# A linear-attention and gated-MLP block: two output transposes joined, gate/up tasks halved, two weight slices moved

## The chip, the cores and the metric

The kernel runs on one core of a Trainium2 chip. The metric is the device time of one execution in microseconds (us), the median of several. The engines are named as the profile names them: PE (TensorE matmul), PEld (its weight loads), DVE (VectorE), ACT (ScalarE), POOL (GpSimd) and SP (SyncE, which here only issues DMAs).

## The reference

Sequence 2048, width 448, 16 heads of 28, inner width 1792, all in bfloat16:

```
n = layernorm(x);  q, k, v = split(n @ wqkv)
phi(t) = where(t > 0, t + 1, exp(t)) + 1e-6
kv = phi(k).T @ v and z = sum(phi(k)), per head
o = (phi(q) @ kv) / (phi(q) @ z + 1e-6)
h = x + o @ wo
m = layernorm(h)
out = h + (gelu(m @ w_gate) * (m @ w_up)) @ w_down
```

## The kernel before, in words

The sequence is cut into 16 tiles of 128 rows. Every piece of work is a task with a name, an engine, the buffers that it reads and writes, and from these its waits. The tasks of an engine run strictly in the order that a table of names, ORDERS (L14), gives for it: one string for PE, ACT, DVE, POOL and SP. A task at the head of its engine's queue that waits holds back everything behind it.

**Attention.** Per tile t: layernorm statistics on DVE (`bnst`, `bnag`), `ln` and `rstd` on ACT, `norm` on DVE or POOL, a transpose (`tr0` to `tr3` on PE with an evacuation `ev` on ACT, later tiles by DMA, `xT`). `k`, `v` (L561) are the two halves of a tile's key and value products; `ek` and `evv` on ACT, a clamp `cl` on POOL (L566) and `ph` on DVE (L568) make phi(k) and v, and `acc` adds the tile to the sum kv, which stays in two banks of PSUM. `qa`, `qb` (L606) are query products of two head groups for four tiles, evacuated by ACT (`eq`, `rq`: exponential and relu, L616, L617) and finished by DVE (`cq`, `pq`). When all tiles are in kv, DVE copies it out (`kz1`, `kz2`).

**From attention to the MLP.** Tiles 0 and 1 go by `a2_first` (L663): `nd` multiplies phi(q) with kv, DVE divides (`rd`, `om`) into `o_sb`, `tro` transposes the tile on PE, `evo` on ACT evacuates it, `wo` multiplies with wo, `hr` on DVE adds x, then layernorm, `trh` (seven transposes of hn on PE) and `evh`. The other tiles go in pairs by `a2_pair` (L711), with DMA transposes `oT` and `hT` on SP instead; DVE adds a copy of hn (`wrap`), and POOL computes the layernorm's factors and the norm.

**MLP.** `gu_chunk` (L788) makes gate and up for 2, 2, 4, 4 and 4 tiles. A task `gu` fills one pair of PSUM banks: two column blocks of 128 for chunks of two tiles, 28 matmuls, or one block for chunks of four, 14 matmuls. The pairs of banks alternate, so gu3 reuses those of gu1. Two `ge` on ACT apply gelu to the gate half, two `hm` on DVE multiply it with up. `down` multiplies two tiles with w_down, `out` adds h, `dout` stores.

**Halves of 64 rows.** Most matmuls contract only 64 rows, in pairs: one on array rows 0 to 63 into one bank, its partner on rows 64 to 127 into another (`pe_pairs`, L434). A task's second half (`v`, `qb`, `nd..b`, `wo..b`, `down..b`) uses the same two banks with the row halves exchanged, so it waits until the first half is complete. Tasks that use all 128 rows are the warm-up `warm0`, `nd0`, `nd1`, `tro`, most of `wo0` and `wo1`, `trh` and the last four tiles' `down`.

**Start.** 16 small and 38 further products of ones run on PE (`warm1`, `warm0`, L457) while the first x tiles arrive; they wait for `ones`, a POOL memset.

**Loads.** SP issues x, weights and DMA transposes from one queue. The gate and up weights come as seven slices of 64 rows each (`dwg0`, `dwu0`, ..., L536), all issued before the first `oT`; the down weights (`dwd`, L732) follow oT2 and oT3. A gate/up task reads slice k with its k-th pair of matmuls.

Of the kernel before, what the change touches and what calls it, by code (L numbers as in the profile page):

```python
# [912 lines left out]
```

## Time and profile before

| | |
|---|---|
| median of 3 runs | 196.69 us (196.25 to 196.73) |
| the profiled execution | 196.7 us |
| its span, first to last instruction | 194.9 us |
| PE busy in the span | 190.3 us (98%) |
| PE's granted clock over the span | 0.999 |
| from the first instruction to the first gate/up product | 54.13 us |

The span is the profiled program's own instructions; 1.8 us of the execution lie around it. In a timeline row stand the start from the span's first instruction, the length from there to the end of the last instruction in the row, engine, line, operation, what is written and read, shapes and count; the brackets tell idle time of the engine ahead of it and what ended it. Consecutive equal instructions share a row, so a step is read as the difference of two starts. Matmul ends overlap the next starts.

### The profile page before, as it was taken

What the parts mean: (1) busy time and instruction counts of PE and PEld (TensorE: products, weight loads), DVE (VectorE), ACT (ScalarE), POOL (GpSimd) and SP (SyncE); (2) the same over time, 40 slices, a digit from 0 to 9 for tenths busy, and PEclk for the clock granted to TensorE, in tenths of its full rate; (3) what the DMA queues carried; (4) which work ended last, traced back from release to release, by engine and by line L of the source; (5) the groups of instructions that cost most, each with busy time, mean ns of one, the idle gap of its engine ahead of it and who ended that gap; (6) DMA issues with size and microseconds to landing.
All of it is one profiled execution on the core that took longest, in us unless ns stands there. A gap on an engine that the chain in (4) does not pass through costs nothing.

```text
span 194.9 us, 5336 instructions
## 1 busy us (share of the span) xinstructions
PE 190.3 (98%) x2192; PEld 137.9 (71%) x2192; DVE 116.3 (60%) x301; ACT 78.2 (40%) x205; POOL 42.0 (22%) x90
## 2 busy tenths in 40 slices
PE   7999999999999999999999999999999999999994
PEld 7556658754588977976675577877778779899554
DVE  2989735368998946843967745756735443431512
ACT  3689866669784212220442441233232442411100
POOL 3099974300050310500500500500500000000000
PEclk9999999999999999999999999999999999999999
DMA  6944558999836052152062250172040000010111
GB/s 191 377 116 97 81 110 185 247 248 205 260 103 110 15 101 50 50 105 62 10 129 46 46 106 2 30 117 51 5 94 28 23 0 0 3 47 3 47 47 47
DMA packets 37256, 17.53 MB, mean 90 GB/s; under 512 B 28272, under 2 KB 36336, under 8 KB 37232
## 3 DMA queue, kind: packets, MB, share of 16 engines
q1 hardware_dynamic: 36352, 16.45, 36.8%
q10 hardware_dynamic: 880, 0.75, 1.2%
q8 instruction: 17, 0.28, 0.6%
q14 instruction: 7, 0.06, 0.1%
HBM read 8.72 MB, written 1.84 MB: 54 GB/s over the span
## 4 chain that ended last, share of the span: by engine, by line
PE 96%; issue 1%; ACT 1%; DVE 1%; POOL 0%; DVEq 0%; ACTq 0%; POOLq 0%
PE ps L430 87%; PE ps L780 6%; PE ps L454 2%; DVE x_sb L660 1%; PE ps L495 1%; ACT xn L617 1%; PE ps L681 0%; ACT xnT L523 0%; PE ps L672 0%; DVE x_sb L756 0%; POOL ones_bf L395 0%; POOL eps_t L398 0%; ACT pqT L616 0%; DVEq L196 0%; ACTq L196 0%
## 5 line engine op out<-in xcount | busy, mean ns | idle before, releaser
L430 PE MATMUL ps<-hnT,wgu_sb 64*128 64x512 bf16 (+1 forms) x980 | 90.4, 333 | 0.0
L430 PEld LDWEIGHTS ps<-hnT,wgu_sb 64*128 64x128 bf16 x980 | 64.5, 94 | 18.6 <-DVE hh L832 1.7
L830 ACT ACTIVATE gl<-ps 128x256 bf16<-128x256 f32 x112 | 36.9, 381 | 89.3 <-PE ps L430 88.2
L832 DVE TENSOR_TENSOR hh<-ps,gl 128x256 bf16<-128x256 f32 x112 | 42.5, 415 | 35.7 <-ACT gl L830 31.5
L430 PE MATMUL ps<-wd_sb,hh 64*128 64x448 bf16 x336 | 34.4, 349 | 0.0
L430 PEld LDWEIGHTS ps<-wd_sb,hh 64*128 64x128 bf16 x336 | 25.6, 94 | 6.2 <-DVE x_sb L756 0.2
L430 PE MATMUL ps<-wkv_sb,xnT 64*128 64x448 bf16 x192 | 22.4, 350 | 0.4 <-ACT xnT L523 0.4
L462 DVE BATCH_NORM_STATS2 st<-x_sb 128x6 f32<-128x448 bf16 x32 | 18.7, 611 | 2.6 <-DMA x_sb<-in_A_x_dram 2.6
L756 DVE TENSOR_TENSOR x_sb<-ps,x_sb 128x448 bf16<-128x448 f32 (+1 forms) x17 | 9.9, 591 | 16.6 <-PE ps L430 9.8
L474 POOL TENSOR_SCALAR ln<-mv 128x2 f32<-128x2 f32 x7 | 1.6, 223 | 75.0 <-DVE mv L463 74.9
L568 DVE SCALAR_TENSOR_TENSOR pk<-ps,tm 128x448 bf16<-128x448 f32 x16 | 9.8, 620 | 9.6 <-POOL tm L566 7.1
L430 PE MATMUL ps<-xnT,wq_sb 64*128 64x512 bf16 x112 | 14.9, 377 | 0.2 <-ACT xn L617 0.2
L430 PEld LDWEIGHTS ps<-wkv_sb,xnT 64*128 64x128 bf16 x192 | 10.1, 94 | 6.3 <-issue 0.8
L430 PE MATMUL ps<-wo_sb,oT 64*128 64x448 bf16 x98 | 12.1, 350 | 0.1
L660 DVE TENSOR_TENSOR x_sb<-ps,x_sb 128x448 bf16<-128x448 f32 x16 | 9.4, 618 | 4.6 <-PE ps L430 4.4
L780 PE MATMUL ps<-wd_sb,hh 128*128 128x448 bf16 (+1 forms) x70 | 10.8, 315 | 0.0
L566 POOL TENSOR_SCALAR tm<-e 128x448 bf16<-128x448 bf16 x16 | 8.9, 559 | 6.4 <-ACT e L565 5.5
L487 POOL TENSOR_SCALAR hn<-x_sb,nm,rs 128x448 bf16<-128x448 bf16 x14 | 10.0, 720 | 0.8 <-POOL rs L476 0.2
L565 ACT ACTIVATE e<-ps 128x448 bf16<-128x448 f32 x16 | 8.5, 541 | 3.5 <-PE ps L430 2.2
L780 PEld LDWEIGHTS ps<-wd_sb,hh 128*128 128x128 bf16 x70 | 6.7, 98 | 4.3 <-issue 0.4
L655 DVE TENSOR_TENSOR o_sb<-ps,rd 128x448 bf16<-128x448 f32 x16 | 9.4, 612 | 0.1
L570 ACT ACTIVATE v<-ps 128x448 bf16<-128x448 f32 x16 | 8.4, 542 | 2.1 <-PE ps L430 2.1
(69 smaller groups left out, 140.4 us busy)
## 6 DMA issues: line engine op xcount, KB each, us to landing
out_dram<-x_sb SPq DMA_DIRECT2D x15, 112.0 KB, 1.7
wgu_sb<-in_B_w_gate_dram SPq DMA_DIRECT2D x7, 224.0 KB, 6.1
wgu_sb<-in_B_w_up_dram SPq DMA_DIRECT2D x7, 224.0 KB, 6.4
wd_sb<-in_B_w_down_dram SPq DMA_DIRECT2D x1, 1568.0 KB, 8.3
x_sb<-in_A_x_dram SPq DMA_DIRECT2D x2, 448.0 KB, 5.3
wkv_sb<-in_A_wqkv_dram ACTq DMA_DIRECT2D x2, 336.0 KB, 3.7
x_sb<-in_A_x_dram SPq DMA_DIRECT2D x3, 224.0 KB, 4.2
wo_sb<-in_A_wo_dram SPq DMA_DIRECT2D x2, 336.0 KB, 4.4
```

Source lines behind the costliest of these rows:

```text
L430: ins = e.matmul(o_, l_, r_, start=s_, stop=p_, **kw)
L462: op("dve", lambda e: e.bn_stats(st[:, t, :], src_ap), [b_src], [b_st[t]], "%sbnst%d" % ("" if mv is mv1 else "h", t), 0.53, key, after=after)
L487: return lambda e: e.tensor_scalar(dst, src[:, t, :], nm[:, t:t + 1], rs[:, t:t + 1], ALU.add, ALU.mult)
L565: act_exp(lambda e: e.activation(e1[:, ie, :], oK, AF.Exp), bank(bk), [b_e1[ie]], "ek%d" % t, _c_act(D), kk)
L566: op("pool", lambda e: e.tensor_scalar(tm1[:, ie, :], e1[:, ie, :], 1.0 + EPS, 0.0, ALU.min, ALU.max), [b_e1[ie]], [b_tm1[ie]], "cl%d" % t ...
L568: op("dve", lambda e: e.scalar_tensor_tensor(pk[:, i, :, 0:GW], psK3, EPS, tm1[:, ie, :].rearrange("p (g e) -> p g e", g=NG), ALU.max, ALU ...
L655: op("dve", lambda e: e.tensor_tensor(o_sb[:, so, oc:oc + D].rearrange("p (a e) -> p a e", e=28), nd3[:, :, 0:28], rd[:, i, :].unsqueeze(2 ...
L660: op("dve", lambda e: e.tensor_tensor(h_sb[:, u, :], ps[:, b, 0:D], x_sb[:, u, :], ALU.add), bank(b) + [b_x[u]], [b_h[u]], "hr%d" % u, 0.5 ...
L756: op("dve", lambda e: e.tensor_tensor(x_sb[:, t, c0:c1], ps[:, bk, c0:c1], h_sb[:, t, c0:c1], ALU.add), bank(bk) + [b_h[t]], [bo], "out%d% ...
L780: ins = e.matmul(ps[:, bk, c0:c1], hh[:, j, hsl(t)], wd_sb[:, j, c0:c1], start=(j == 0), stop=(j == NJ - 1))
L830: G.add("act", lambda e, gi=gi, cs_=cs_, psG=psG: e.activation(gl[:, gi, cs_], psG[:, cs_], AF.Gelu_apprx_tanh), r=bank(BK_G[i]), w=[b_glh ...
L832: op("dve", lambda e, dst=dst, srcU=srcU, srcL=srcL: e.tensor_tensor(dst, srcU, srcL, ALU.mult), bank(BK_U[i]) + [b_glh], [b_ar[j_][t % HR ...
```

## The change

- `tro0` and `tro1` become one task (`tro_first`): sixteen transposes in eight 64-row pairs. Rows 0 to 63 of both tiles go to one bank, rows 64 to 127 to the other. The task waits for `om0` and `om1`; `evo0` and `evo1` each read both banks and wait for all sixteen.
- A gate/up task of two column blocks becomes two tasks, a and b, of 14 matmuls each, in the same order of matmuls. `ge` and `hm` still wait for the second.
- Slices 5 and 6 of the gate and up weights are issued behind oT2 and oT3, and the down weights behind those.
- `trh` waits for the wrap copy only at its seventh transpose, the one that reads it.
- Clamps `cl14` and `cl15` run on DVE instead of POOL. `warm0` has 33 products instead of 38.
- ORDERS is a new table. At the start, `ones` on POOL stands behind `eps`, `mhalf` and `opad` (a memset of `o_sb`) instead of first; `rstd3` on ACT stands behind `ek0` and `ln4`, `tr3` on PE behind `v1`. In the hand-over, `qb31` stands behind the hn transposes instead of between `wo2a` and `wo2b`, and `cq14` on DVE behind `hm3`. In the last chunk gu54 and gu55 stand behind both halves of down10.

PE around the o transposes, before (the rows are nd2a, tro0, nd2b, then qb30 with qa21, tro1, qb21; kvz with pqT is `nd`, wq_sb is `qa` or `qb`):

```order
L430 MATMUL ps<-kvz,pqT 128x116 x8
L681 MATMUL ps<-ident,o_sb 128x128 x4
L430 MATMUL ps<-kvz,pqT 128x116 x8
L430 MATMUL ps<-xnT,wq_sb 128x512 x14
L681 MATMUL ps<-ident,o_sb 128x128 x4
L430 MATMUL ps<-xnT,wq_sb 128x512 x6
```

The same place of the changed kernel, up to the first products of wo1:

```order
L433 MATMUL ps<-kvz,pqT 128x116 x8
L693 MATMUL ps<-ident,o_sb 128x64 x16
L433 MATMUL ps<-kvz,pqT 128x116 x8
L433 MATMUL ps<-xnT,wq_sb 128x512 x20
L709 MATMUL ps<-wo_sb,oT 128x448 x3
```

The second group of o transposes is gone from between qa21 and qb21, and the sixteen stand where the first four did.

PE from qa31 to the fourth gate/up task, before (wo_sb is `wo`, ident with hn is `trh`, wgu_sb is `gu`):

```order
L430 MATMUL ps<-xnT,wq_sb 128x512 x8
L430 MATMUL ps<-wo_sb,oT 128x448 x8
L430 MATMUL ps<-xnT,wq_sb 128x512 x6
L430 MATMUL ps<-wo_sb,oT 128x448 x6
L702 MATMUL ps<-ident,hn 128x128 x14
L430 MATMUL ps<-kvz,pqT 128x116 x16
L430 MATMUL ps<-hnT,wgu_sb 128x256 x140
L430 MATMUL ps<-wo_sb,oT 128x448 x14
L430 MATMUL ps<-hnT,wgu_sb 128x256 x28
```

and in the changed kernel:

```order
L433 MATMUL ps<-xnT,wq_sb 128x512 x8
L433 MATMUL ps<-wo_sb,oT 128x448 x14
L725 MATMUL ps<-ident,hn 128x128 x14
L433 MATMUL ps<-xnT,wq_sb 128x512 x6
L433 MATMUL ps<-kvz,pqT 128x116 x16
L433 MATMUL ps<-hnT,wgu_sb 128x256 x140
L433 MATMUL ps<-wo_sb,oT 128x448 x8
L433 MATMUL ps<-hnT,wgu_sb 128x256 x14
L433 MATMUL ps<-wo_sb,oT 128x448 x6
```

wo2a and wo2b are now adjacent, qb31 (the six wq_sb products) follows the hn transposes, and half of gu4 stands between wo4a and wo4b.

DVE between the evacuation of hnT (`evh1`) and the products of the first two gate/up tasks, before (rd and o_sb are tiles 4 and 5, hh is `hm`, the row on pqT is `cq14`):

```order
L709 COPY hnT<-ps 128x7x128
L618 TENSOR_SCALAR pqT<-pqT 112x2x512
L462 BN_STATS st<-x_sb 128x6
L654 RECIPROCAL rd<-ps 128x16
L462 BN_STATS st<-x_sb 128x6
L654 RECIPROCAL rd<-ps 128x16
L463 BN_AGGR mv<-st 128x2 x2
L655 TENSOR_TENSOR o_sb<-ps,rd 128x448
L832 TENSOR_TENSOR hh<-ps,gl 128x256 x2
L655 TENSOR_TENSOR o_sb<-ps,rd 128x448
L832 TENSOR_TENSOR hh<-ps,gl 128x256 x2
```

and in the changed kernel:

```order
L732 COPY hnT<-ps 128x7x128
L465 BN_STATS st<-x_sb 128x6 x2
L466 BN_AGGR mv<-st 128x2
L662 RECIPROCAL rd<-ps 128x16 x2
L466 BN_AGGR mv<-st 128x2
L663 TENSOR_TENSOR o_sb<-ps,rd 128x448 x2
L857 TENSOR_TENSOR hh<-ps,gl 128x256 x4
```

cq14 has left, and om4 now stands ahead of the products of gu1 instead of between those of gu1 and gu0.

The diff, cut to its core:

```
-    "warm1 warm0 tr0 tr1 k0 v0 k1 tr2 tr3 v1 k2 acc0a k3 v2 v3 qa00 acc0b acc1b qb00 k4 acc1a acc2a v4 k5 acc2b acc3b"
+    "warm1 warm0 tr0 tr1 k0 v0 k1 tr2 v1 tr3 k2 acc0a k3 v2 v3 qa00 acc0b acc1b qb00 k4 acc1a acc2a v4 k5 acc2b acc3b"
...
+    GU_AHEAD = 5
+    CL_DVE = cfg.get("cl_dve", (14, 15))
-    WARM = 38
+    WARM = 33
...
+        def load_gu(ks, prev, key):
+            for k in ks:
+                prev = [dma(wgu_sb[0:64, k, :], wg3[:, k, :], [b_wg[k]], "dwg%d" % k, 64 * FF * 2, after=prev, key=key)]
+                prev = [dma(wgu_sb[64:128, k, :], wu3[:, k, :], [b_wu[k]], "dwu%d" % k, 64 * FF * 2, after=prev, key=key)]
+            return prev
+        prev = load_gu(range(GU_AHEAD), prev, 20.0)
...
+            op("dve" if t in CL_DVE else "pool", lambda e: e.tensor_scalar(tm1[:, ie, :], e1[:, ie, :], 1.0 + EPS, 0.0, ALU.min, ALU.max),
...
+        def tro_first():
+            P, Q = FIRST_BK[0][1], FIRST_BK[1][1]
+            def ftro(e):
+                ins = None
+                for t in (0, 1):
+                    for k in range(4):
+                        for b, rows in ((P, A_), (Q, B_)):
+                            ins = e.transpose(psb[:, b, (4 * t + k) * 64:(4 * t + k + 1) * 64], o_sb[rows, t % O_R, k * 128:(k + 1) * 128], ident[rows, rows])
+                return ins
+            G.add("pe", ftro, r=[b_o[0], b_o[1], b_ident], w=bank(P, Q), name="tro0", dur=0.054 * 8, key=-19.9, mode=64, rg={P: "A", Q: "B"})
+            for t in (0, 1):
+                tvo = psb[:, P:Q + 1, t * 256:(t + 1) * 256].rearrange("p b (k t) -> p k b t", t=64)
+                ov_ = oT[:, t % O_R, :, :].rearrange("p k (b t) -> p k b t", t=64)
+                op("act", lambda e, tvo=tvo, ov_=ov_: e.activation(ov_, tvo, AF.Identity), bank(P, Q), [b_oT[t % O_R]], "evo%d" % t, _c_act(512), -19.8)
...
                 if u == 3:
-                    dma(wd_sb[:, :, :], B_w_down.rearrange("(j p) n -> p j n", p=128), [b_wd], "dwd", FF * D * 2, key=ka, after=o_ts)
+                    late = load_gu(range(GU_AHEAD, 7), o_ts, ka)
+                    dma(wd_sb[:, :, :], B_w_down.rearrange("(j p) n -> p j n", p=128), [b_wd], "dwd", FF * D * 2, key=ka, after=late)
...
-                pe_pairs("gu%d" % v, both(a, b), N, [b_hnT[t % HR] for t in tiles] + [(x, 2 * k) for k, x in enumerate(b_wg)] + [(x, 2 * k + 1) for k, x in enumerate(b_wu)],
-                         [(b_ps[BK_G[i]], 0), (b_ps[BK_U[i]], 1)], kb, {BK_G[i]: "A", BK_U[i]: "B"})
+                    pe_pairs("gu%d%s" % (v, "ab"[jj] if nj > 1 else ""), both(a, b), N,
+                             [b_hnT[t % HR] for t in tiles] + [(x, 2 * k) for k, x in enumerate(b_wg)] + [(x, 2 * k + 1) for k, x in enumerate(b_wu)],
+                             [(b_ps[BK_G[i]], 0), (b_ps[BK_U[i]], 1)], kb + 0.01 * jj, {BK_G[i]: "A", BK_U[i]: "B"})
```

More of the change, by code (lines that the diff above doesn't have):

```diff
@@ L535, in bass_sequential_preLN__linear_attn_block__glu_gated_geglu__prompt_kernel @@
         prev = [dma(wo_sb[:, 4:7, :], A_wo[64:448, :].rearrange("(g p) n -> p g n", p=128), [b_wo[3]], "dwo_s", 384 * D * 2, after=prev, key=19.0)]
-        for k in range(7):
-            prev = [dma(wgu_sb[0:64, k, :], wg3[:, k, :], [b_wg[k]], "dwg%d" % k, 64 * FF * 2, after=prev, key=20.0)]
-            prev = [dma(wgu_sb[64:128, k, :], wu3[:, k, :], [b_wu[k]], "dwu%d" % k, 64 * FF * 2, after=prev, key=20.0)]
+        def load_gu(ks, prev, key):
[4 more added lines that the diff above has]
+        prev = load_gu(range(GU_AHEAD), prev, 20.0)
         acc_tasks = []
@@ L565, in kv_tile @@
             act_exp(lambda e: e.activation(e1[:, ie, :], oK, AF.Exp), bank(bk), [b_e1[ie]], "ek%d" % t, _c_act(D), kk)
-            op("pool", lambda e: e.tensor_scalar(tm1[:, ie, :], e1[:, ie, :], 1.0 + EPS, 0.0, ALU.min, ALU.max),
-               [b_e1[ie]], [b_tm1[ie]], "cl%d" % t, 0.53, kk)
+            op("dve" if t in CL_DVE else "pool", lambda e: e.tensor_scalar(tm1[:, ie, :], e1[:, ie, :], 1.0 + EPS, 0.0, ALU.min, ALU.max),
+               [b_e1[ie]], [b_tm1[ie]], "cl%d" % t, _c_dve(D, 4.0) if t in CL_DVE else 0.53, kk)
             op("dve", lambda e: e.scalar_tensor_tensor(pk[:, i, :, 0:GW], psK3, EPS, tm1[:, ie, :].rearrange("p (g e) -> p g e", g=NG), ALU.max, ALU.add),
@@ L661, in res_h, with nd_first @@
             ln_stats(u, h_sb[:, u, :], b_h[u], st2, mv2, b_st2, b_mv2, ka)
-        def a2_first(t):
+        def nd_first(t):
             ka = -20.0 + 0.1 * t
-            bnd, bh = FIRST_BK[t]
-            so = t % O_R
+            bnd = FIRST_BK[t][0]
             def fnnd(e):
@@ L675, in a2_first @@
             nd_evac(t, bnd, 0, ka)
-            tvo = psb[:, bh, 0:512].rearrange("p (k t) -> p k t", k=4)
+        def tro_first():
+            P, Q = FIRST_BK[0][1], FIRST_BK[1][1]
             def ftro(e):
                 ins = None
-                for k in range(4):
-                    ins = e.transpose(tvo[:, k, :], o_sb[:, so, k * 128:(k + 1) * 128], ident[:])
-                return ins
-            G.add("pe", ftro, r=[b_o[so], b_ident], w=bank(bh), name="tro%d" % t, dur=_c_mm(128, 4), key=ka)
-            op("act", lambda e: e.activation(oT[:, so, :, :], tvo, AF.Identity), bank(bh), [b_oT[so]], "evo%d" % t, _c_act(512), ka)
+                for t in (0, 1):
+                    for k in range(4):
+                        for b, rows in ((P, A_), (Q, B_)):
+                            ins = e.transpose(psb[:, b, (4 * t + k) * 64:(4 * t + k + 1) * 64], o_sb[rows, t % O_R, k * 128:(k + 1) * 128], ident[rows, rows])
+                return ins
+            G.add("pe", ftro, r=[b_o[0], b_o[1], b_ident], w=bank(P, Q), name="tro0", dur=0.054 * 8, key=-19.9, mode=64, rg={P: "A", Q: "B"})
[3 more added lines that the diff above has]
+                op("act", lambda e, tvo=tvo, ov_=ov_: e.activation(ov_, tvo, AF.Identity), bank(P, Q), [b_oT[t % O_R]], "evo%d" % t, _c_act(512), -19.8)
+        def a2_first(t):
+            ka = -20.0 + 0.1 * t
+            bnd, bh = FIRST_BK[t]
+            so = t % O_R
             def fnwo(e):
@@ L696, in a2_first, with ftrh @@
             tvh = psb[:, bh, 0:896].rearrange("p (k t) -> p k t", k=7)
-            def ftrh(e):
+            def ftrh(e, W):
                 ins = None
-                for k in (0, 1, 2, 4, 5, 6, 3):
+                for n, k in enumerate((0, 1, 2, 4, 5, 6, 3)):
+                    if n in (0, 6):
+                        W(n)
                     ko = k * 128 if k < 4 else (k - 4) * 128 + 64
@@ L703, in ftrh @@
                 return ins
-            G.add("pe", ftrh, r=[b_hn[sh], b_hnd[sh], b_ident], w=bank(bh), name="trh%d" % t, dur=_c_mm(128, 7), key=ka)
+            G.add("pe", ftrh, r=[b_hn[sh], (b_hnd[sh], 6), b_ident], w=bank(bh), name="trh%d" % t, dur=_c_mm(128, 7), key=ka, mw=True, pdt=_c_mm(128))
             hv_ = hnT[:, :, (t % HR) * 128:(t % HR + 1) * 128]
@@ L802, in gu_chunk @@
                 psU = ps[:, BK_U[i], 0:W_]
-                a, b = [], []
                 for jj in range(nj):
                     j = j0 + jj
+                    a, b = [], []
                     for k in range(7):
@@ L837, in gu_chunk @@
             vcount[0] = v
+        for t in (0, 1):
+            nd_first(t)
+        tro_first()
         done = 0
```

91 rows, old and new, of the table ORDERS are left out of this document.

## The prediction

> **What bounds the kernel now.** I read the page first, then the table of stretches, then the timeline engine by engine where PE has gaps. The page:
>
> ```profile
> span 194.9 us, 5336 instructions
> PE 190.3 (98%) x2192; PEld 137.9 (71%) x2192; DVE 116.3 (60%) x301; ACT 78.2 (40%) x205; POOL 42.0 (22%) x90
> ```
>
> PE is busy for 98% of the span, so the time moves only where PE's own stream becomes shorter or where PE waits. The stretch of the gate/up and down products (columns: stretch, its length, busy time of PE, PEld, DVE, ACT, POOL, then clock, DMA share, GB/s):
>
> ```profile
> 54.13:181.65 127.52, 127.40 (x1488) 98.36 (x1481) 75.18 (x203) 38.31 (x112) 17.84 (x35) 1.00 0.24 50
> ```
>
> Two thirds of the span have no idle PE. What is left to win is in the hand-over from the attention part, between about 41 and 54 us, and in small drains inside the dense part. Here is PE in the hand-over (columns: start, length, instructions):
>
> ```profile
> 43.48 0.38 PE L430 MATMUL ps<-kvz,pqT 64*128 64x116 bf16 x8
> 43.78 0.40 PE L681 MATMUL ps<-ident,o_sb 128*128 128x128 bf16 x4
> 44.11 0.38 PE L430 MATMUL ps<-kvz,pqT 64*128 64x116 bf16 x8
> 44.33 1.68 PE L430 MATMUL ps<-xnT,wq_sb 64*128 64x512 bf16 x14
> 45.94 0.40 PE L681 MATMUL ps<-ident,o_sb 128*128 128x128 bf16 x4
> 46.27 0.82 PE L430 MATMUL ps<-xnT,wq_sb 64*128 64x512 bf16 x6
> ...
> 49.21 1.04 PE L430 MATMUL ps<-xnT,wq_sb 64*128 64x512 bf16 x8 [0.19 <-ACT xn L617]
> 50.07 0.94 PE L430 MATMUL ps<-wo_sb,oT 64*128 64x448 bf16 x8
> 50.83 0.83 PE L430 MATMUL ps<-xnT,wq_sb 64*128 64x512 bf16 x6
> 51.48 0.75 PE L430 MATMUL ps<-wo_sb,oT 64*128 64x448 bf16 x6
> 52.16 0.95 PE L702 MATMUL ps<-ident,hn 128*128 128x128 bf16 x14
> 53.04 0.22 PE L430 MATMUL ps<-kvz,pqT 64*128 64x116 bf16 x1
> 53.47 0.82 PE L430 MATMUL ps<-kvz,pqT 49*128 49x116 bf16 x15 [0.21 <-DVE x_sb L660]
> ```
>
> Three things stand in it. The fourteen hn transposes take 52.16 to 53.04, 0.063 each, and four o transposes take 43.78 to 44.11, 0.33; four at 0.06 are 0.23, so a change between 128-row and 64-row work costs about 0.1. At 49.21 PE waits for ACT, and at 53.47 for DVE (0.43 after the first nd4 product).
>
> **The change, part by part.** *The o transposes.* Each of the two L681 tasks stands between 64-row tasks. As 64-row pairs they lose four changes of mode. Sixteen transposes in eight pairs: no row has them alone. Below, half the columns at half of 0.063 are 0.03 a pair, 0.25 in all; above, the x transposes (9.76 in the fence on the start) took 0.75 for ten pairs, changes of shape among them, so 0.6. I take 0.25, since all sixteen have one shape, and keep 0.6 for a rival. What follows is set by ACT as well:
>
> ```profile
> 43.74 1.02 ACT L617 ACTIVATE xn<-ps 112x1024 bf16<-112x1024 f32 x1
> 44.64 0.60 ACT L684 ACTIVATE oT<-ps 128x512 bf16<-128x512 bf16 x1
> ...
> 48.05 1.93 ACT L617 ACTIVATE xn<-ps 112x1024 bf16<-112x1024 f32 x2
> ```
>
> Now, from nd2a at 43.48: nd2a 0.22 (as nd2b, 44.11 to 44.33), transposes 0.25, nd2b 0.22, qb30 0.65 (as qb31, 50.83 to 51.48), which gives 44.82. qa21 writes the banks that the rq6 row (43.74 to 44.76) reads; with 0.14 from ACT's end to PE (the first 48.05 activation ends near 49.07, qa31 starts at 49.21) it starts at 44.90, takes 0.86 as qa31 does, and qb21 starts at 45.76 instead of 46.27. What follows up to qa31, wo1, wo0, eq10 and rq10, hangs on qb21 as before, so qa31 comes at 48.70 instead of 49.21: **-0.51**. The two evacuations of o, at 44.64 and right behind, end near 45.7, in time for wo1; eq12 is 0.5 later behind them, but eq10 waits for qb21 anyway.
>
> *qb31 moved behind the hn transposes.* Before, qa31 to the first gate/up product took 49.21 to 54.13, 4.92. Now: qa31 0.86, wo2a 0.76, a drain, wo2b with its change 0.68, transposes 0.88, qb31 0.65, nd4a and nd4b 0.66. The drain is new, because wo2b uses wo2a's two banks with the row halves exchanged and nothing stands between. Its price is in the next rows, where the fourteen wo4 products stand alone:
>
> ```profile
> 54.13 7.89 PE L430 MATMUL ps<-hnT,wgu_sb 64*128 64x256 bf16 x140
> 61.77 1.81 PE L430 MATMUL ps<-wo_sb,oT 64*128 64x448 bf16 x14
> 63.42 0.82 PE L430 MATMUL ps<-hnT,wgu_sb 64*128 64x256 bf16 x12
> ```
>
> From 61.77 to 63.42 are 1.65, against 0.76 and 0.57 for the halves: 0.32. The sum is 4.81, **-0.11**, gu1 at 53.51. The 0.43 wait for DVE at nd4a goes only if hr3 is early enough, which the DVE rows below decide: hr2 and hr3 (52.26, 1.16) can start 0.64 earlier, when the wrap ahead of them ends, and end near 52.78; nd4a arrives at 52.85. It is covered, with nothing to spare.
>
> *Gate/up tasks in two.* The matmuls and their order are the same; a half can now stand between wo4a and wo4b, and does. This removes the 0.32 drain of the last fence: **-0.32**. wo10a and wo10b stay adjacent.
>
> *What is late next: DVE.* The third gate/up task, gu3, reuses gu1's banks, so it waits for both hm1 products:
>
> ```profile
> 51.95 0.18 DVE L695 COPY hn<-hn 128x64 bf16<-128x64 bf16 x1
> 52.26 1.16 DVE L660 TENSOR_TENSOR x_sb<-ps,x_sb 128x448 bf16<-128x448 f32 x2
> ...
> 53.87 0.42 DVE L618 TENSOR_SCALAR pqT<-pqT 112x1024 bf16<-112x1024 bf16 x1
> 54.20 0.62 DVE L462 BATCH_NORM_STATS2 st<-x_sb 128x6 f32<-128x448 bf16 x1
> ...
> 55.64 0.62 DVE L655 TENSOR_TENSOR o_sb<-ps,rd 128x448 bf16<-128x448 f32 x1
> 56.35 0.75 DVE L832 TENSOR_TENSOR hh<-ps,gl 128x256 bf16<-128x256 f32 x2
> ```
>
> hm1 ended at 57.10 and gu3 came at 54.13 plus two of 1.53 (140 products, five tasks, 7.64), 57.19: DVE was already just in time. Now DVE's queue starts 0.51 earlier, loses cq14 (53.87 to 54.20, 0.33) and two waits (52.13 to 52.26, 56.27 to 56.35, 0.2), and gains om4 ahead of hm1 (0.55 by its step in a queue). hm1 ends at 57.10 - 0.51 - 0.33 - 0.2 + 0.55 = 56.61, and gu3, arriving at 56.57, starts at about 56.7: **+0.1**, between 0 and 0.5.
>
> *The start.* Five warm-up matmuls go, but the memset that they wait for now stands behind a longer one:
>
> ```profile
> 0.99 0.31 POOL L403 MEMSET o_sb<- 128x256 bf16 x1
> 1.93 4.24 PE L454 MATMUL ps<-ones_bf 128*128 128x128 bf16 x38
> 6.10 0.96 PE L495 MATMUL ps<-ident,xn 64*128 64x64 bf16 x20
> 7.43 0.74 PE L430 MATMUL ps<-wkv_sb,xnT 64*128 64x448 bf16 x6 [0.36 <-ACT xnT L523]
> 9.20 0.54 ACT L565 ACTIVATE e<-ps 128x448 bf16<-128x448 f32 x1 [0.54 <-PE ps L430]
> 9.76 0.75 PE L495 MATMUL ps<-ident,xn 64*128 64x64 bf16 x20
> 10.35 1.08 ACT L523 ACTIVATE xnT<-ps 128x512 bf16<-128x512 bf16 x2
> ```
>
> Five of 0.11 are -0.55, the memsets +0.4, so k0 comes about 0.15 earlier. It is given back at k2, which needs the evacuation at 10.35: ACT's queue from ek0 (9.20) to it has one rstd more, 0.1 to 0.2. I take **0**, with -0.15 and +0.2 as ends.
>
> *At nothing:* clamps 14 and 15 on DVE instead of POOL (the last acc tasks did not wait for them visibly, and kz starts when the same products end); wqz later (wq is read some us behind it); the wrap wait at the seventh hn transpose; the gate/up order after gu20 (evacuations of ACT and DVE fit under PE there: 38 and 75 of 127 us); gu54 and gu55 side by side before down12, which reads them as the last two of fourteen steps.
>
> *Gate/up slices 5 and 6 behind oT2 and oT3.* The page's data rate by slice and its line on the down weights, the landing times in the view of the tile oT, and two rows of SP's timeline (start, length of the issue):
>
> ```profile
> GB/s 191 377 116 97 81 110 185 247 248 205 260 103 110 15 101 50 50 105 62 10 129 46 46 106 2 30 117 51 5 94 28 23 0 0 3 47 3 47 47 47
> wd_sb<-in_B_w_down_dram SPq DMA_DIRECT2D x1, 1568.0 KB, 8.3
> DMA to landing us min/median/max: 2.4/2.5/4.2
> ...
> 45.48 2.51 SPq L729 DMA_TRANSPOSE oT<-o_sb  x2
> 56.29 3.53 SPq L729 DMA_TRANSPOSE oT<-o_sb  x2
> ```
>
> Four loads of 229 KB at 248 GB/s (slices 7 and 8, 34 to 44 us) are 3.7 us. They are issued when oT3 has been, before at 47.99, now some 0.2 sooner as om2 is; they flow behind it from about 49 and are in by 52.7; the sixth and seventh pairs of gu1 want them at 54.1. No wait, with 1.4 to spare. The down weights move from about 49.4 to 52.7 and end by 59.2 (1.6 MB at 248 GB/s); oT4 and oT5, issued 0.5 to 1 us earlier than 56.29, land by about 60, and wo4a, three gate/up tasks behind gu3, wants them at 56.7 + 4.6 = 61.3.
>
> **The sum.** -0.51 - 0.11 + 0.1 - 0.32 = -0.84. The profiled execution took 196.7 around its span of 194.9, the same as the median of the runs, 196.69. 196.7 - 0.84 is **195.9**.
>
> **Rivals.** *DVE takes it back.* With om4 and om5 both ahead of hm1, gu3 may come where it came, at 57.19; then only the wo4 drain is saved: 196.4. For it: DVE has no slack in those rows. Against: its queue starts earlier and lost cq14.
>
> *The o transposes don't get cheaper.* At 0.6 for the eight pairs qa21 starts 0.25 later: 196.1.
>
> *The transposes of tiles 4 and 5 wait for the down weights (slower).* If everything on SP's queue passes in order and keeps the distances it had, the down weights, issued at 47.99, land 3.7 later, at 47.99 + 8.3 + 3.7 = 60.0, and oT5 3.7 later than before. There its issue began near 57.6, so it landed between 60.1 and 61.8, now 63.8 to 65.5. wo4a then waits about 3 us: 195.9 + 3 = 198.9. It decides the sign once oT5 lands later than about 62.1. Against: before, the down weights landed at 56.3 and oT4 was issued at 56.29, so it did not wait for them, and by the sum above the queue keeps over 1 us of slack. The Trainium skill, "DMA: Bandwidth & Descriptors", section "Queues, rings and completion order", says that on each DMA engine descriptors are taken in ring order. By that rule the moved loads stay ahead of oT4, and this rival's 198.9 is what it gives if the slack is too small; the trace of before shows no case of it on its own.
>
> *The clock opens late (slower).* The warm-up products took 0.11 each, the hn transposes of the same size 0.063: the early ones ran at half pace. The ten pairs of x transposes took 0.96 at 6.10 and 0.75 at 9.76. If the shorter, later warm-up leaves k0, v0 and k1 at half pace, eleven pairs cost their 0.19 (wo2a: four in 0.76) once more: +2, 197.9. Against: the first dense product is only 0.15 earlier, and PE is as busy in the 4 us before it. The Trainium skill, "TensorE: Matmul & The Clock Gate", part 1, says that the gate opens after a busy window of some 3.4 us that runs free of the kernel's start; by this rule a late opening could fall on any run, before the change too.
>
> **Chances.** Forecast 0.53; DVE 0.19; transposes 0.08; late oT5, small (within 1 us) 0.06 and large 0.08; clock 0.06. About 0.3% (0.6 us) is what a measurement of this kernel can tell from no change. Faster by more: the forecast and a little of the transposes, 0.55; slower: large late oT5 and clock, 0.14; the rest, 0.31. The range goes from 195.3 (start -0.15, gu3 0, some luck) to 197.0, which leaves out the two slow cases and little below.
>
> **What would show it.** In the changed profile: sixteen o transposes of 64 rows within 0.3 us and no 0.1 gaps around them; qa31 near 48.7; gu1 near 53.5; gu3 about 3.2 behind gu1; no extra 0.32 between wo4a and wo4b; k2 near 11.0. I am wrong if PE idles ahead of wo4a or inside gu1 (a DMA), or if gu3 is more than 3.5 behind gu1 (DVE).

## The result, and the profile after

The changed kernel takes **197.16 us** in the median of 8 executions (196.78 to 199.25), the kernel before 196.56 beside it (196.15 to 196.73). The ratio is 1.0054, with a 95% interval from 1.0031 to 1.0076: slower, where the prediction said faster. (The ratios here lie close to those of the mean times; the two medians alone give 1.003.)

The profiled execution is the fastest of the eight, 196.78, so its trace shows less than the typical loss. Of its page, the span, the engines, the data rate by slice and the chain:

```profile
span 195.0 us, 5340 instructions
PE 189.6 (97%) x2195; PEld 124.3 (64%) x2195; DVE 117.4 (60%) x303; ACT 77.6 (40%) x205; POOL 41.1 (21%) x88
GB/s 187 372 136 86 58 108 135 266 250 71 239 310 123 3 57 56 115 124 27 3 138 34 54 98 0 37 69 0 50 174 16 3 24 3 0 0 0 3 71 94
PE 89%; DMA 4%; DVE 3%; SPq 1%; ACT 1%; issue 1%; DVEq 0%
```

PE's work did become shorter, 189.6 us instead of 190.3, but the chain that ended last now holds 4% of DMA, where it held none, and the tenth slice (44 to 49 us) moves 71 GB/s where it moved 205. PE in the hand-over of the changed kernel:

```profile
43.31 0.37 PE L433 MATMUL ps<-kvz,pqT 64*128 64x116 bf16 x8
43.52 0.40 PE L693 MATMUL ps<-ident,o_sb 64*128 64x64 bf16 x16
43.75 0.38 PE L433 MATMUL ps<-kvz,pqT 64*128 64x116 bf16 x8
43.97 2.60 PE L433 MATMUL ps<-xnT,wq_sb 64*128 64x512 bf16 x20
48.70 1.04 PE L433 MATMUL ps<-xnT,wq_sb 64*128 64x512 bf16 x8 [0.19 <-ACT xn L625]
49.55 1.74 PE L433 MATMUL ps<-wo_sb,oT 64*128 64x448 bf16 x14
51.23 0.96 PE L725 MATMUL ps<-ident,hn 128*128 128x128 bf16 x14
52.11 0.82 PE L433 MATMUL ps<-xnT,wq_sb 64*128 64x512 bf16 x6
52.77 0.82 PE L433 MATMUL ps<-kvz,pqT 64*128 64x116 bf16 x16
53.43 0.92 PE L433 MATMUL ps<-hnT,wgu_sb 64*128 64x256 bf16 x13
54.79 7.18 PE L433 MATMUL ps<-hnT,wgu_sb 64*128 64x256 bf16 x127 [0.44 <-DMA wgu_sb<-in_B_w_up_dram]
```

The sixteen o transposes take 43.52 to 43.75, nd4 no longer waits, and gu1 comes at 53.43 instead of 54.13. Then it stops after 13 of its first 14 matmuls. The fourteenth belongs beside the thirteenth, at 54.08; it came at 54.79, and all behind it is 0.60 late. What it waited for is the last load of the slices, in the view of the weights' tile at that one issue:

```profile
L367 SPq DMA_DIRECT2D wgu_sb<-in_B_w_up_dram x1: 602/602/602, 49.6 to 49.6; - x1
  PE ps L433: 0.4, 1
DMA to landing us min/median/max: 5.2/5.2/5.2
```

Issued at 49.6, landed 5.2 later, near 54.75. SP's timeline of the changed kernel shows when the late loads are issued (start, length of the issue):

```profile
38.50 0.60 SPq L367 DMA_DIRECT2D wgu_sb<-in_B_w_up_dram  x1
45.12 2.51 SPq L752 DMA_TRANSPOSE oT<-o_sb  x2
47.67 0.59 SPq L367 DMA_DIRECT2D wgu_sb<-in_B_w_gate_dram  x1
49.58 0.60 SPq L367 DMA_DIRECT2D wgu_sb<-in_B_w_up_dram  x1
50.22 0.59 SPq L367 DMA_DIRECT2D wd_sb<-in_B_w_down_dram  x1
```

And the table of stretches shows what the DMA engines did meanwhile (the last three columns are granted clock, DMA share and GB/s):

```profile
44.00:46.00 2.00, 1.94 (x24) 0.62 (x20) 1.90 (x6) 2.00 (x4) 0.00 (x0) 1.00 0.12 29
49.00:50.00 1.00, 1.00 (x14) 0.54 (x12) 1.00 (x3) 0.46 (x2) 0.00 (x0) 1.00 1.07 283
50.00:51.00 1.00, 0.94 (x12) 0.26 (x8) 0.97 (x6) 0.71 (x4) 0.00 (x0) 1.00 0.80 262
51.00:52.00 1.00, 1.00 (x18) 0.78 (x14) 0.97 (x4) 0.74 (x1) 0.00 (x0) 1.00 1.01 246
52.00:53.00 1.00, 1.00 (x18) 0.56 (x15) 1.00 (x4) 0.78 (x1) 0.00 (x0) 1.00 0.89 212
53.00:54.00 1.00, 0.94 (x26) 0.75 (x21) 1.00 (x3) 1.00 (x2) 0.00 (x0) 1.00 1.05 268
54.00:55.00 1.00, 0.56 (x11) 0.27 (x7) 1.00 (x6) 0.98 (x2) 0.32 (x2) 1.00 1.07 358
```

From 44 to 46 the DMA engines stand nearly still (share 0.12), since SP waits for `om2` with the loads behind it. From 49 on the four loads' 917 KB would be through by 52.6 (283 + 262 + 246 and 0.6 of 212). But by 54.74 some 1540 KB had moved: about 620 KB, nearly all of it down weights, issued behind, passed before slice 6 was reported in. The Trainium skill, "DMA: Bandwidth & Descriptors", section "Queues, rings and completion order", says that one copy is split over up to 16 engines, each with its own ring, and that completion is not in order across them; the trace agrees in that bytes of the later copy came before the last ones of slice 6.

The DMA packets that the trace holds tell what was late. A slice travels in packets of 3584 bytes, 256 for the four loads, and 250 of them had ended by 53.0. The last four ran one directly behind the other, from 52.63 to 53.78. The first of them began as a packet of 16 KB of the instruction queue (q8 on the page) ended, which had run from 51.40 to 52.65. In e4 below that packet ran from 52.66 to 53.88, and four slice packets followed it one by one from 53.87 to 54.96, when all others had ended by 53.38. In e2, with two late loads, the last slice packet ended at 51.34, just as the instruction packet began. So the late share looks like one DMA engine that was held by an instruction fetch and still had its slice packets to move. The records name no engine and no run moved the fetch, so this is read and not tested. From the end of the last slice packet to the product that wants it another 1.0 us passes (53.78 to 54.79).

**Where the rest went.** The distances between landmarks on PE, in us, of single profiled executions (e2, e9 and e13 are experiments below):

| from, to | before | after | e2 | e9 | e13 |
|---|---|---|---|---|---|
| k0, k2 | 3.59 | 3.71 | 3.71 | 3.71 | 3.61 |
| k2, nd2a | 32.46 | 32.60 | 32.60 | 32.59 | 32.40 |
| nd2a, gu1 | 10.66 | 10.11 | 10.11 | 10.11 | 10.11 |
| gu1, gu5 | 6.11 | 6.72 | 6.19 | 6.20 | 6.20 |
| gu5, down0a | 8.18 | 7.88 | 7.88 | 7.88 | 7.85 |
| down0a, gu15 | 22.83 | 23.01 | 23.01 | 23.01 | 23.01 |
| gu15, wo12b | 27.07 | 27.04 | 27.05 | 27.04 | 27.04 |
| wo12b, down12 | 63.33 | 63.64 | 63.65 | 63.50 | 63.50 |

Where the order is the same, the rows behind nd2a mostly repeat to 0.02 between executions. The two rows at the start spread more: k0 to k2 takes 3.59 to 3.61 in four traces with the old order there and 3.71 in the fifth (e12), and 3.71 in all with the new order but e6's (4.98, below); k2 to nd2a takes 32.59 to 32.65 with the new order. k0 itself comes anywhere from 6.82 to 7.63. So the change gives 0.55 in the hand-over and 0.30 at wo4, and takes back 0.14, 0.18 and 0.31 in three places of the new order, and 0.12 ahead of k2 that e12 does not let us put down to the order. All this is before the late slice is counted: gu3 comes 3.67 behind gu1 against 3.05 in e2, of which 0.08 is made up by gu5 (6.72 against 6.19).

The 0.14 between k2 and nd2a is lost at once: k4 comes 4.64 behind k2 instead of 4.50. In the new order the weight loads of acc0a wait there, in the view of PEld's waits (us in total, times, longest):

```profile
PEld ps L433 <- DVE wq_sb L415: 0.4, 1, 0.4
```

L415 is `wqz`, a memset that the new order puts behind ph0; acc0a does not read it. All ten traces with the new order at the start have this wait; those of the kernel before, e3, e10, e12 and e13 have not. What exactly acc0a waits for stays open.

### The profile page after: what moved, and what is told of

Read it like the earlier page. It is cut to its first block, busy times and chain, and to the rows that moved or that the text cites. A ratio compares the mean times of both kernels' runs of the same rounds, so it can differ in the third digit from the quotient of the medians.

```text
span 195.0 us, 5340 instructions
## 1 busy us (share of the span) xinstructions
PE 189.6 (97%) x2195; PEld 124.3 (64%) x2195; DVE 117.4 (60%) x303; ACT 77.6 (40%) x205; POOL 41.1 (21%) x88
## 4 chain that ended last, share of the span: by engine, by line
PE 89%; DMA 4%; DVE 3%; SPq 1%; ACT 1%; issue 1%; DVEq 0%
PE ps L433 83%; PE ps L804 6%; DMA wgu_sb<-in_B_w_up_dram 3%; DMA x_sb<-in_A_x_dram 2%; SPq L367 1%; DVE o_sb L663 1%; DVE pqT L626 1%; ACT pqT L624 1%; PE ps L498 0%; DVE st L465 0%; DVE pqT L627 0%; PE ps L679 0%; DVE rd L662 0%; SPq L752 0%; DVE xn L489 0%
## 5 line engine op out<-in xcount | busy, mean ns | idle before, releaser
L433 PE MATMUL ps<-hnT,wgu_sb 64*128 64x512 bf16 (+1 forms) x980 | 91.7, 333 | 0.4 <-DMA wgu_sb<-in_B_w_up_dram 0.4
L433 PEld LDWEIGHTS ps<-hnT,wgu_sb 64*128 64x128 bf16 x980 | 55.0, 94 | 30.6 <-DVE hh L857 4.3
L433 PE MATMUL ps<-wd_sb,hh 64*128 64x448 bf16 x336 | 35.2, 349 | 0.0
L433 PEld LDWEIGHTS ps<-wd_sb,hh 64*128 64x128 bf16 x336 | 23.9, 94 | 7.9 <-DVE hh L857 0.3
L433 PE MATMUL ps<-wkv_sb,xnT 64*128 64x448 bf16 x192 | 23.0, 350 | 0.1
L484 POOL TENSOR_SCALAR nm<-mv 128x2 f32<-128x2 f32 x13 | 2.9, 227 | 39.3 <-DVE mv L466 38.9
```

The lines of the kernel that those rows point to most:

```text
L433: ins = e.matmul(o_, l_, r_, start=s_, stop=p_, **kw)
```

## The experiments

### Where slices 5 and 6 go

e1 puts both slices ahead of oT2 and oT3 again in the changed kernel, e2 only slice 5. e3 is the kernel before with nothing but the late slices. e8 makes slice 4 late as well.

```
e1:  ... dwg4 dwu4 dwg5 dwu5 dwg6 dwu6 oT2 oT3 dwd        GU_AHEAD = 7
e2:  ... dwg4 dwu4 dwg5 dwu5 oT2 oT3 dwg6 dwu6 dwd        GU_AHEAD = 6
e3:  ... dwg4 dwu4 oT2 oT3 dwg5 dwu5 dwg6 dwu6 dwd        (kernel before)
e8:  ... dwg3 dwu3 oT2 oT3 dwg4 dwu4 dwg5 dwu5 dwg6 dwu6 dwd   GU_AHEAD = 4
```

> The changed kernel with slices 5 and 6 of the gate and up weights issued ahead of oT2 and oT3 again, all else as changed. Theory (late slices): in the changed kernel PE stood 0.60 us inside gu1, from 54.19 to 54.79, because the last up slice landed at 54.74; in the unprofiled executions, 0.4 longer in the median than the profiled one, this wait is longer. Here that slice lands near 48.5, the wait is gone, gu1 runs through, and the time is 197.16 less 0.6 to 1.0: 196.2 to 196.6. wo2a then wants oT2 and oT3 at 49.55, and they land near 49.4, so up to 0.3 of it may come back there. Rival (the gain is lost elsewhere, in the start or the last chunk): 197.0 to 197.3, as the changed kernel.

> The changed kernel with slice 5 ahead of oT2 and oT3 and only slice 6 behind them. Theory (late slices): two loads fewer stand between oT3 and the last up slice, which lands about 1.3 to 2 us sooner than 54.74, near 53.0, and gu1's seventh pair wants it at 54.1, so no wait; oT2 and oT3 land before 49.4, in time for wo2a at 49.55: 196.0 to 196.5, the same as or a little below the kernel with all slices ahead. If one slow DMA engine makes the landing vary by more than 1 us, a part of the wait stays: 196.6 to 197.0. Rival (the gain is lost elsewhere): 197.0 to 197.3.

> The kernel before with nothing changed but the four loads of slices 5 and 6, issued behind oT2 and oT3, and the down weights behind them. Theory (late slices): the first late load is issued near 48.0 (after oT3's issue), 0.35 later than in the changed kernel, and the last lands near 55.1, while gu1, at 54.13, wants it at 54.8: a wait of 0.2 to 0.6 inside gu1 and a time of 196.8 to 197.2 against 196.56. Rival (the late slices are harmless): within 0.1 of the kernel before.

> The changed kernel with slice 4 as well behind oT2 and oT3: six loads stand there instead of four. Theory (the stall in gu1 is the landing of the late loads): each pair of loads adds 1.3 (two issues of 0.64) to 1.85 us (two of 229 KB at 248 GB/s) to the landing of the last slice, which comes at 56.0 to 56.6 instead of 54.74, and gu1 waits 1.3 to 1.9 longer: 198.4 to 199.1. Rival (the stall has another cause, for example a fixed delay behind the transposes): 197.1 to 197.5, as with four loads.

| | median us | range (executions) | ratio to before, 95% |
|---|---|---|---|
| e1 | 197.42 | 197.17 to 198.60 (6) | 1.0056 [1.0038, 1.0075] |
| e2 | 196.46 | 196.18 to 197.91 (12) | 1.0010 [0.9991, 1.0029] |
| e3 | 197.24 | 196.84 to 198.86 (12) | 1.0041 [1.0025, 1.0057] |
| e8 | 200.66 | 198.99 to 200.75 (4) | 1.0183 [1.0147, 1.0219] |

e3 alone shows it: the late slices by themselves cost the old kernel 0.6 between the medians (197.24 against 196.60 beside it), in its trace a wait inside gu1 that ends at 55.23. e2 removes the wait, and with it the loss, but no measurable gain is left: its interval holds 1. e1 missed its expectation. Its gu1 does not wait, but wo2 does, in PE's timeline:

```profile
48.92 1.04 PE L433 MATMUL ps<-xnT,wq_sb 64*128 64x512 bf16 x8 [0.19 <-ACT xn L625]
50.35 2.19 PE L433 MATMUL ps<-wo_sb,oT 64*128 64x448 bf16 x14 [0.39 <-DVE st L465]
52.48 0.95 PE L725 MATMUL ps<-ident,hn 128*128 128x128 bf16 x14
```

The view of the tile oT at the issues of oT2 and oT3 (45.35 and 46.60) has their landing:

```profile
DMA to landing us min/median/max: 4.1/4.5/4.9
```

wo2a starts 1.43 behind qa31 instead of 0.85, and its two halves take 2.13 instead of 1.68: 1.0 in all. The row names DVE, whose `st` is no input of wo2; the transposes land at 50.26 and 50.69, behind the seven slices (the last lands at 49.73). In the kernel before the last slice landed 7.5 behind its issue at 40.91, near 48.4, and oT2 and oT3 near 49.0 and 49.3. So in these traces the slices ahead make oT late, and the slices behind are late themselves; one slice on each side fits.

e8 went past its expectation, 3.5 more instead of 1.2 to 1.9. Its PE timeline inside gu1:

```profile
55.23 0.28 PE L433 MATMUL ps<-hnT,wgu_sb 64*128 64x256 bf16 x1 [0.69 <-DMA wgu_sb<-in_B_w_up_dram]
56.06 0.28 PE L433 MATMUL ps<-hnT,wgu_sb 64*128 64x256 bf16 x1 [0.55 <-DMA wgu_sb<-in_B_w_gate_dram]
56.99 5.18 PE L433 MATMUL ps<-hnT,wgu_sb 64*128 64x256 bf16 x62 [0.65 <-DMA wgu_sb<-in_B_w_up_dram]
```

Its table of stretches, with the granted clock third from the end:

```profile
56.00:57.00 1.00, 0.29 (x3) 0.11 (x4) 0.00 (x0) 0.00 (x0) 0.93 (x2) 0.97 1.09 329
58.00:59.00 1.00, 1.00 (x14) 0.72 (x10) 0.00 (x0) 0.09 (x1) 0.00 (x0) 0.50 1.08 379
60.00:61.00 1.00, 1.00 (x18) 0.82 (x16) 0.15 (x1) 0.48 (x1) 0.00 (x0) 0.82 1.02 146
61.00:62.00 1.00, 1.00 (x22) 0.88 (x20) 0.29 (x1) 0.66 (x2) 0.00 (x0) 1.00 0.33 60
```

The waits grew, by a little more than the theory said: gu1a's last product, the fourteenth, comes at 56.99, 2.2 later than with four loads. But PE had run three products in 3 us, and the granted clock fell to 0.50: 0.97 and 0.82 in the first and the third row put the fall at 56.94 and the return at 60.36, 3.4 later, which costs another 1.7 (half of 3.4). The Trainium skill, "TensorE: Matmul & The Clock Gate", part 1, gives this gate with its window of about 3.4 us; the trace agrees. In e3 the execution of 198.86 is the one of twelve with a mean clock of 0.991, as three of e8's four have. The fourth, with a mean clock of 1.000, took 198.99, inside the expectation.

### The stream of loads

In e1 the loads started late as well: the last xT was issued at 28.60 instead of 27.37, and the new table has norm15 behind two other tasks on POOL. e5 is e1 with norm15 back.

```
- cl7 norm14 cl8 powwarm opad2 norm15 cl9
+ cl7 norm14 opad2 norm15 cl8 powwarm cl9
```

> All slices ahead of oT2 and oT3, and on POOL opad2 and norm15 ahead of cl8 and powwarm, as in the kernel before. Theory: with all slices ahead wo2a stood from 49.78 to 50.35 and wo2b until 51.80, because oT2 and oT3 landed at 50.26 and 50.69, behind a stream of loads that started 1.8 us later than before (norm15 ended at 27.64 instead of 26.22, so the last xT and every weight load behind it came later). With norm15 back, the stream starts 1.3 to 1.8 us sooner, oT3 lands near 49.4 as before, wo2a does not wait: 197.42 less 0.9 to 1.1, 196.3 to 196.5. Rival (oT2 and oT3 are late for another reason, the issue or the bandwidth): 197.2 to 197.5.

196.96 (196.16 to 197.72, 12 executions), ratio 1.0024 [1.0008, 1.0040]: half of what was expected. In its trace, of an execution of 197.48, the last xT is issued at 28.57 all the same (SP's own queue holds it), the last slice lands at 49.72 as in e1 (49.73), and oT2 and oT3 at 50.27 and 50.69. So norm15 is not what makes this execution's stream late. What the median gained was in executions that have no trace; three of them took less than 196.6, so all slices ahead are not late every time. What starts the stream late in the others stays open.

### The order of the last chunks

e4 is the changed kernel with the order of the kernel before from gu28 on, on every engine; e6 the same on e2, e7 on e5.

```
- ... wo12b gu28 nd14a gu29 nd14b down4b gu30 gu31 down6a gu33 wo14a gu32 wo14b down6b gu35 ...
+ ... wo12b gu29 nd14a gu28 nd14b gu31 down4b gu30 gu33 gu32 wo14a gu35 wo14b gu34 gu37 gu36 down6a ...
```

> The changed kernel with the order of the kernel before on every engine from gu28 on (last two chunks of gate/up and down). Theory: between gu43 and down12 the changed kernel lost 0.25 in waits of about 0.05 of a gate/up task for hm; with the old order these go and the time is 0.2 to 0.3 lower than the changed kernel's 197.16, near 196.9, still behind the kernel before. Rival (the last chunk loses nothing that is not noise): 197.1 to 197.2. Second rival (the whole loss lies here): 196.3 to 196.6.

> Only slice 6 behind oT2 and oT3, and from gu28 on the order of the kernel before on every engine. With slice 6 alone late the time was 196.46; between wo12b and down12 it took 63.65 in its trace against 63.33 before and 63.50 with the old order of the last chunks in the changed kernel. Theory: the old order gives 0.15 to 0.3 back: 196.15 to 196.3. Rival (those waits are not of the order): 196.4 to 196.5.

> All slices ahead, norm15 early, and the order of the kernel before from gu28 on: the rest of the change alone, without its two late streams. Theory: 0.15 to 0.3 less than with the changed order of the last chunks, 196.0 to 196.3, faster than the kernel before by 0.3 to 0.6, which is what is left of the 0.84. If oT3 still lands after 49.7, wo2a keeps a wait and it is 196.4 to 196.8.

e4: 197.27 (197.03 to 197.85, 6), no gain over the changed kernel. e6: 196.25 (196.01 to 198.00, 12), 0.2 below e2. e7: 197.12 (196.24 to 199.57, 12), a miss, no better than e5, and oT3 lands at 50.43 in its trace. From wo12b to down12 the old order takes 63.50 in e4, e6 and e7 against 63.65: it gives back half of the 0.31; the other half stays with the old order and is not explained. In that stretch (146 to 184 us) weight loads wait for `hm` in the changed kernel, in the view of waits (us in total, times, longest):

```profile
PEld ps L433 <- DVE hh L857: 2.9, 9, 0.4
```

and before:

```profile
PEld ps L430 <- DVE hh L832: 0.6, 3, 0.2
```

In e4's profiled execution (197.85) the gain was hidden by a still later landing of the late slice:

```profile
53.74 0.92 PE L433 MATMUL ps<-hnT,wgu_sb 64*128 64x256 bf16 x13
56.04 4.21 PE L433 MATMUL ps<-hnT,wgu_sb 64*128 64x256 bf16 x74 [1.38 <-DMA wgu_sb<-in_B_w_up_dram]
```

Up to gu28 this is the changed kernel. The last slice was issued at 49.9 and landed 6.1 later, against 5.2: the wait is 1.5 instead of 0.6. A spread of this size can be why the changed kernel's median lies 0.4 above its profiled execution; the other executions have no trace.

### The start

e6's profiled execution took 198.0, while ten of its twelve took 196.0 to 196.5. Its first products on PE (x transposes, k0, then v0 with k1):

```profile
6.29 0.54 PE L498 MATMUL ps<-ident,xn 64*128 64x64 bf16 x10 [0.35 <-DVE xn L489]
7.08 0.54 PE L498 MATMUL ps<-ident,xn 64*128 64x64 bf16 x10 [0.25 <-DVE xn L489]
7.63 1.30 PE L433 MATMUL ps<-wkv_sb,xnT 64*128 64x448 bf16 x6
9.36 1.83 PE L433 MATMUL ps<-wkv_sb,xnT 64*128 64x448 bf16 x12
```

and those of the changed kernel's profiled execution:

```profile
5.79 0.41 PE L498 MATMUL ps<-ident,xn 64*128 64x64 bf16 x10
7.00 0.74 PE L433 MATMUL ps<-wkv_sb,xnT 64*128 64x448 bf16 x6
8.00 1.31 PE L433 MATMUL ps<-wkv_sb,xnT 64*128 64x448 bf16 x12
```

k0's six products take 1.30 instead of 0.74: half pace, up to about 10.4. This is the fourth rival of the prediction. x came 0.5 later, the short warm-up had ended, PE stood 0.35 and 0.25, and the pace did not open. The view of stretches reads a granted clock of 1.00 here, because the trace has no clock record ahead of its first one; that first record, of full clock, begins at 10.46 here, and between 3.80 and 7.00 in the twelve other traces that have one (5.64 in the changed kernel's). That the idle time kept the clock down is argued from this one trace. e9 is e6 with the start of the kernel before, e10 the kernel before with the short start.

```
e9:   ones first on POOL,                       WARM = 38   (on e6)
e10:  eps mhalf opad ones ident mones ...,      WARM = 33   (on the kernel before)
```

> As the kernel with slice 6 alone late and the old order of the last chunks, but with the start of the kernel before: 38 warm-up products and the memset of ones first. In the profiled execution of that kernel (198.0) the warm-up ended near 5.7, the x transposes waited for xn until 6.29, and k0, v0 and k1 ran at half pace (k0's three pairs 0.35 each instead of 0.19), 1.6 lost by k2; the other executions took 196.0 to 196.5. Theory (clock): executions of 197.6 and more, 2 in 12 there and 2 in 8 of the changed kernel, come from this and vanish, in 12 of 12 below 197.2; the median stays at 196.1 to 196.4. Rival (they come from late loads): still 2 or so of 12 above 197.5.

> The kernel before with 33 warm-up products instead of 38 and the memset of ones behind eps, mhalf and opad, nothing else. Theory (clock): median within 0.2 of the kernel before (196.3 to 196.7), but 1 to 3 of about 10 executions at 197.7 to 199, because there k0, v0 and k1 run at half pace. Rival (the slow executions come from late loads, the start is harmless): all executions between 196.1 and 197.2, like those of the kernel before.

e9: 196.28 (196.09 to 196.54, 11), ratio 0.9996 [0.9987, 1.0005]. e10: 196.37 (196.13 to 197.99, 11), ratio 1.0006 [0.9989, 1.0022], one execution far off and the other ten up to 196.63. Over 197.5 are 5 of the 24 executions of e2 and e6 and one of e10's; none of the 41 of e9, e11, e12 and e13, which have the long start, and none of the kernel before in any comparison (at most 197.22). Among kernels with the short start, the changed kernel has two far off (198.60 and 199.25 of 8) and e7 four (198.75 to 199.57 of 12), e5 none of 12 (at most 197.72). So the short start wins less than 0.1 in most executions and seems to lose 1.4 to 1.8 in one of five to ten. Only e6's 198.0 has a trace. For the others the cause is argued: e2 and e6 ran on one chip, e9 to e11 on another, e12 and e13 on two more, so the long start was not run beside e2 and e6, and e10 beside the kernel before is one execution of 11 against none of 27.

### The o transposes alone

e11 is e9 with the joined task in eight 128-row transposes.

```
-    for t in (0, 1):
-        for k in range(4):
-            for b, rows in ((P, A_), (Q, B_)):
-                ins = e.transpose(psb[:, b, (4 * t + k) * 64:(4 * t + k + 1) * 64], o_sb[rows, ...], ident[rows, rows])
+    for t, b in ((0, P), (1, Q)):
+        for k in range(4):
+            ins = e.transpose(psb[:, b, k * 128:(k + 1) * 128], o_sb[:, ...], ident[:])
```

> As the kernel with the start back, but the o transposes of tiles 0 and 1, still one task, in eight 128-row transposes instead of sixteen of 64 rows. Theory (the pairs of 64 rows are cheaper by their pace and the two changes of mode): the task takes 8 of 0.063 and two changes of 0.1, 0.70, instead of 0.23; qa21 comes up to 0.47 later and so does gu1: 0.3 to 0.5 more than with the pairs. Rival (something else holds qa21 and qa31 there, ACT's rq6 and rq10, and the pairs win nothing): within 0.1 of it.

196.71 (196.43 to 196.94, 11), 0.43 more than e9, as expected. The task and nd2b behind it:

```profile
43.85 0.62 PE L692 MATMUL ps<-ident,o_sb 128*128 128x128 bf16 x8
44.40 0.38 PE L433 MATMUL ps<-kvz,pqT 64*128 64x116 bf16 x8
```

0.55 for the eight against 0.23 for the sixteen (43.52 to 43.75 above), and 0.1 for the change of mode ahead of them (nd2a at 43.54 is 0.31 ahead of 43.85, above it is 0.21). It passes to the end nearly whole. (The two evacuations read one bank each here, instead of both.)

### What is left

e12 keeps the hand-over, the halved tasks and slice 6 alone late, and takes everything up to qa11 and from gu28 on from the kernel before; pq14 moves behind out2. e13 puts pq14 directly behind hm12.

```
changed:  hm13_0 pq14 wrap6 hm12_0 hm13_1 hm12_1 out2 hr9 hr8
e12:      hm13_0 wrap6 hm12_0 hm13_1 hm12_1 out2 pq14 hr9 hr8
e13:      hm13_0 wrap6 hm12_0 hm13_1 hm12_1 pq14 out2 hr9 hr8
```

> What the accounting leaves of the change: the hand-over from qa11 on and the halved gate/up tasks as changed, slice 6 alone late; from the kernel before the whole first phase on every engine (start, order of v1 and the acc tasks, clamps on POOL) and the order from gu28 on; on DVE pq14 moved behind out2, so that hm12 and hm13 come sooner. Theory: against the kernel with the start back (196.28) this saves 0.12 between k0 and k2, 0.14 between k2 and nd2a (an exchange of row halves in the acc tasks) and 0.14 at down2a (28 products in 2.79 instead of 2.65, waiting for hm): 195.8 to 196.0, 0.5 less than the kernel before. Rival (these differences of single traces are noise): 196.2 to 196.4.

> As the kernel of the gains only, with pq14 on DVE directly behind hm12, where DVE stood idle from 85.9 to 90.2, instead of behind out2. There PE waited 0.48 at 92.5 for hr9 and hr8, which stood behind pq14; up to that wait PE was 0.73 ahead of the kernel before. Theory (the accounting of single traces holds): the 0.48 goes and the time is 195.85 to 196.05, ratio near 0.997 to 0.998, faster than the kernel before. Rival (those 0.73 were luck of one execution): 196.3 to 196.4 again.

e12: 196.40 (196.06 to 196.69, 11), ratio 1.0000 [0.9991, 1.0009], a miss of its own making. Up to gu15 it was 0.73 ahead of the kernel before; then nd10a waited for hr9 and hr8, behind pq14:

```profile
92.51 0.38 PE L433 MATMUL ps<-kvz,pqT 64*128 64x116 bf16 x8 [0.31 <-DVE x_sb L668]
```

e13: **195.82** (195.68 to 196.20, 8), ratio 0.9973 [0.9962, 0.9984], faster than the kernel before beside it, and with it than the changed kernel (1.0054 in its own comparison). Its page:

```profile
span 194.0 us, 5349 instructions
PE 94%; DMA 2%; issue 1%; DVE 1%; ACT 1%; SPq 0%; DVEq 0%
```

The table above accounts for it: +0.02 - 0.06 - 0.55 + 0.09 - 0.33 + 0.18 - 0.03 + 0.17 = -0.51, and the medians differ by 0.52. That they agree to 0.01 is luck, since the first row alone spreads by 0.1. One part of the reading fell: down2a, 2.65 before, still takes 2.79 with hm12 ahead of pq14. What costs that 0.14 stays open.

## Why the prediction was wrong, point by point

**Slices 5 and 6, "No wait, with 1.4 to spare": failed, and this alone made the kernel slower.** The bytes were through when the sum said, by 52.6, but gu1 waits for the last share of the last load, which came 2.1 later, and 1.2 later again in e4's execution. The sum took bytes over the mean rate for the landing. The trace of before had the better price, in the view of the weights' tile, for the same loads:

```profile
DMA to landing us min/median/max: 4.9/6.2/7.7
```

They had landed 4.9 us behind their issue at the soonest. The prediction has oT3's issue done near 47.8; four issues 0.64 apart put the last one near 49.7, so by this price it lands at 54.6 or later, and gu1 wants it at 54.1. Issued at 49.6, it landed near 54.75. The step cost 0.5 in the profiled execution, 1.5 in e4's, and 0.6 to 0.7 in the medians (e3 against the kernel before; the changed kernel against e2). Without it (e2) the change is worth nothing that can be measured. It was named as the place where I would be wrong ("inside gu1 (a DMA)"), but had no price and no chance among the rivals.

**"At nothing": failed.** The new order costs 0.14 behind k2, where acc0a waits for DVE (the prediction put `wqz` later "at nothing"; the view names it), 0.18 in the stretch around down2a, and 0.31 in the order after gu20, said to fit under PE. Busy shares of 38 and 75 in 127 us say nothing of it. A gate/up task of four tiles waits for the `hm` of the task before last. Where the gate/up tasks follow closely, that `hm` ends 1.66 to 1.70 behind the start of its task's last product (before 1.58 to 1.67), and the task between covers about as much. So 0.05 more, whose cause is not shown, is paid again and again. Together 0.63, three quarters of the forecast; e13, which undoes about half of it and the late slice, comes to 195.82.

**The o transposes, -0.51 at qa31: right in mechanism, half as much again as measured.** They take 0.23 as taken (0.25), and e11 shows 0.43 for the pairs. But with tro1 gone qa21 and qb21 stand side by side on the same banks with the row halves exchanged, and lie 1.10 apart instead of 0.86, which the sum left out: qa31 comes 5.39 behind nd2a instead of 5.73, a gain of 0.34. That it stood at 48.70, as predicted, is luck: that execution reached nd2a 0.17 earlier.

**qb31 behind the hn transposes, -0.11: right in sign.** qa31 to gu1 is 4.73 (forecast 4.81, before 4.92), nd4's wait is gone. The hand-over as a whole gained 0.55 of the 0.62.

**wo4, -0.32: right.** gu5 to down0a became 0.30 shorter.

**gu3, +0.1: not seen.** gu1 to gu3 is 3.05 in e2, 3.06 before; DVE did not take it back, and the rival that said so is out. The small loss in gu1 to gu5 (0.09) lies between gu3 and gu5.

**The start, 0: right for most executions, wrong for some.** k0 comes at 6.82 to 7.63 in the traces with the short start and at 6.98 to 7.43 in those with the long one, so no earlier k0 is shown; e10's median is 0.08 below the kernel before. The late clock, a rival at 0.06, is seen in e6's trace and argued for some other executions. It does not move the median, but widens the spread.

**oT4 and oT5 behind the down weights: did not happen.** wo4a came at 61.70 without a wait; oT5, issued at 56.45, had landed 4.7 later.

## What to carry to other kernels

A load is in when its last share is in: price a load that a product needs soon by the time from issue to landing that the trace shows, with its spread, not by bytes over rate, and leave the spread as slack. A new table of orders has a price of its own: compare every place where two tasks on the same two banks become neighbours, and every chain that is as long as the work it hides under. A warm-up has to reach the first dense product in the execution where its input comes latest, not in the median one; this last point rests on one trace.
